# One hand-ordered queue of 513 work units, ordered anew in an attention and maxout feed-forward kernel

## The chip, the cores and the metric

The kernel runs on one core of one Trainium2 chip. The metric is device time in microseconds for one execution, the median of the runs shown. A profile is one further execution, recorded instruction by instruction.

## What is computed

Two stages in one kernel. The first is attention with batch 4, 8 heads, 768 positions and 64 channels per head. A query sees a key if the key is one of the first 8 positions ("global") or lies 0 to 95 positions behind it ("local"); a head's slope times the distance is taken off the score. The second stage multiplies each token (3072 of them, 512 channels) by three weight matrices, keeps the largest of the three products, and multiplies by a fourth matrix.

```python
scores = scale * np.matmul(q, k.transpose(0, 1, 3, 2))
keep = is_global | is_local
dist = np.where(is_global & ~is_local, float(n_local), np.abs(rel))
scores = np.where(keep, scores - slopes * dist, -1e9)
a = softmax(scores)
x = (a @ v) as [B*S, H*D]
h = np.maximum(np.maximum(x @ w1, x @ w2), x @ w3)      # 512 -> 768
out = h @ w_out                                          # 768 -> 512
```

## The kernel before

The 3072 tokens are 24 tiles of 128 (6 per batch entry). A tile's scores reach only its own keys and those of the tile before it, and the 8 global keys are copied over the first 8 columns of the earlier key tile. exp runs without a maximum; the distance and the mask are one multiplication of exp(scores) by exp(-slope x distance), from a table `wmask` built at the start (units K, one per head). V carries a column of ones, so that one matmul gives sum and denominator.

The feed-forward stage works on eight chunks: four of 2 tiles, then four of 4. For each chunk there are 18 groups F (6 blocks of 128 hidden channels times 3 matrices), each four accumulating matmuls into one PSUM buffer; ScalarE copies the first matrix's product out (j = 0), VectorE takes the maximum with the second (j = 1) and the third (j = 2). O is the second matmul of a tile, with its copy and its store.

Nothing in the kernel chooses an order at run time. A string, `SCHEDULE`, lists 513 units, and a loop issues them one after the other. An engine executes its own instructions in that order, so a unit waits for everything that stands ahead of it on its engine. A unit is a letter and numbers. The last number of many units says which engine does the copy or the multiplication: 0 ScalarE, 1 VectorE, 2 GpSimd. In `u_m` it is different, (VectorE, GpSimd) by 0 and 1:

```python
mul = (nc.vector, nc.gpsimd)[how].tensor_mul
```

The units that this text speaks of:

- `l n.s` loads a part of q or k for a group of tiles, `c n.s.e` casts it to bf16, `x n.s.e` transposes it on PE and copies it out of PSUM. Group 0 is the first four tiles in eight parts: 0 to 3 are q of head pairs 0 to 3, called q0 to q3 here, 4 to 7 are k, called k0 to k3. `L`, `C T.0`, `X` do the same for the tiles from 12 on, one tile at a time, with the transpose by DMA (last number 4) or on PE.
- `v T` loads V, `C T.1.e` casts it. `w`, `o` load weights, `W g.j.e` and `Q` cast them. All loads are issued by SP in the order of the list.
- For the first four tiles scores are made for a head pair: `s tp.jp.b` (tp 0: tiles 0 and 1; tp 1: tiles 2 and 3) is PE's scores in PSUM buffer b and ScalarE's exp, `m tp.jp.e` the mask multiplication (L344 with 768 elements per partition for tp 0, L342 with 1024 for tp 1), `g` small copies of global key columns.
- For later tiles `S T.g` and `M T.g` do the same by half of the heads (the multiplication is L360).
- `A T.b` is attention times V and the division on VectorE; with b = 2 in two halves (two PSUM buffers of the three that feed-forward groups use, two reciprocals and two divisions of half the size), else in one. `T T.e` transposes the result for the feed-forward stage, on PE with a copy by e, or by DMA (4). `G` and `V` copy global columns of K and V for a tile.
- `D b.n` issues n matmuls on zeros. `E` is the last chunk's second matmul.

The PSUM pool of the feed-forward groups (`psH`) has three buffers, which T, D and the A units with b = 2 take too, in turn; `psS` has one buffer for each of b = 0 and 1, and `psT` one.

Of the kernel before, what the change touches and what calls it, by code (L numbers as in the profile page):

```python
# [22 lines left out]


SCHEDULE = """
    K0 l0.6 K4 K2 c0.6.2 x0.6.1 K3 K5 l0.0 c0.0.2 x0.0.3 l0.4 c0.4.2 K1 x0.4.4 l0.2 c0.2.1 x0.2.3 l0.1
    g2.0.1 K7 s0.0.1 c0.1.2 s0.2.0 l0.5 c0.5.1 x0.5.4 l0.3 l0.7 c0.7.1 x0.1.3 c0.3.2 g2.2.1 K6 g1.2.2
    g1.0.2 g2.1.1 x0.3.2 x0.7.3 s0.1.1 s0.3.0 g1.1.2 s1.0.1 m0.2.0 s1.2.0 w0.0.0 g1.3.1 g2.3.1 s1.3.1 v0
    C0.1.1 m0.3.0 m0.1.0 m0.0.0 A0.2 m1.0.0 s1.1.0 v1 C1.1.2 m1.3.0 W0.0.0 A1.1 m1.1.0 m1.2.1 D5.6 T0.0
    V1.2 T1.1 v2 C2.1.2 A2.2 V2.0 F0.0.0 v3 C3.1.2 G0.0 A3.1 V3.0 w1.0.0 W2.0.2 w0.1.0 T2.0 F0.4.0  # L30
    F0.1.0 T3.0 F0.5.0 W1.0.1 W0.1.2 F0.1.1 w0.2.0 W0.2.2 l1.0 c1.0.2 G3.0 F1.0.0 F1.0.1 F1.1.0 F1.1.1
    F1.2.0 F0.1.2 F0.2.0 l1.1 c1.1.1 x1.0.2 F0.0.1 F0.0.2 x1.1.4 F1.1.2 F1.4.0 S4.0 S4.1 G4.2 F1.0.2
    F1.3.0 F1.5.0 S5.0 w1.1.0 W2.1.2 M4.0 M4.1 F0.5.1 F0.4.1 M5.0 l2.0 c2.0.0 F1.5.1 S5.1 v5 v4 C4.1.0
    W1.1.2 F0.2.1 F1.3.1 F1.4.1 M5.1 F0.3.0 x2.0.0 l2.2 c2.2.1 A4.1 w1.2.1 W1.2.0 C5.1.2 F0.3.1 x2.2.2
    F1.2.1 V4.2 A5.1 T4.1 F1.3.2 F0.2.2 S7.0 l2.3 T5.1 F1.2.2 F0.3.2 W2.2.2 F1.5.2 F2.0.0 F2.3.0 c2.3.1
    F2.1.0 x2.3.0 M7.0 F0.4.2 F2.4.0 F2.3.1 l2.1 c2.1.2 x2.1.4 F2.5.0 F2.1.1 v6 G6.0 C6.1.1 v8 C8.1.2
    S6.0 l3.0 c3.0.2 S6.1 F2.0.1 M6.0 F2.4.1 M6.1 F2.2.0 S7.1 F0.5.2 v7 C7.1.0 F1.4.2 M7.1 A6.0 F2.5.1
    x3.0.0 F2.2.1 A7.1 F2.2.2 o1 v9 T6.0 o2 Q2.2 F2.1.2 G7.0 F2.4.2 S8.1 S8.0 T7.1 F2.5.2 F2.3.2 F3.0.0
    F3.3.0 M8.0 F3.1.0 F3.4.0 F3.1.1 Q1.2 M8.1 G8.0 F3.2.0 S9.1 C9.1.1 S9.0 F3.4.1 F2.0.2 F3.1.2 V7.2
    G9.2 A8.1 l3.1 c3.1.2 v11 o0 v10 F3.5.0 x3.1.4 L12 C12.0.2 F3.0.1 L15 v15 L13 Q0.0 F3.2.1 M9.1 S10.0  # L40
    S10.1 F3.0.2 O0.1.0 L14 F3.5.1 F3.4.2 F3.2.2 M9.0 M10.0 C15.0.3 C13.0.3 V8.0 G10.0 S11.1 T8.4 S11.0
    O1.1.0 C11.1.0 X12.0 X13.4 L19 A9.1 F3.3.1 M10.1 O2.1.1 V9.2 C10.1.2 v12 C14.0.2 O0.0.0 M11.0 T9.0
    A10.1 O2.0.1 M11.1 S12.0 S12.1 G12.0 X14.4 V10.2 L16 T10.1 F3.5.2 F3.3.2 X15.4 v13 v14 L18 S13.0
    C12.1.2 S13.1 A11.2 O3.0.1 C15.1.2 M12.0 M12.1 T11.0 O3.1.1 G13.0 C19.0.1 F4.0.0 F4.0.1 F4.3.0
    F4.5.0 M13.0 A12.1 F4.5.1 S14.0 S14.1 T12.4 M14.0 M13.1 M14.1 C16.0.2 F4.4.0 F4.4.1 F4.4.2 G14.0
    S15.0 X16.4 M15.0 S15.1 F4.1.0 F4.0.2 C13.1.2 A13.0 T13.4 V13.0 M15.1 F4.2.0 F4.1.1 C14.1.2 A14.0
    V14.1 G15.2 O1.0.0 T14.4 F4.3.1 A15.1 C18.0.1 F4.2.1 V15.0 F4.2.2 F4.5.2 F4.1.2 S16.0 S16.1 G16.1
    M16.1 F4.3.2 T15.4 F5.0.0 F5.3.0 F5.3.1 F5.0.1 F5.5.0 F5.5.1 X18.4 X19.4 S19.1 S18.0 M18.0 v18 L17
    F5.2.0 F5.5.2 C17.0.1 v19 L21 M16.0 C18.1.1 F5.2.1 v16 C16.1.2 F5.2.2 F5.0.2 S18.1 M18.1 S19.0
    F5.1.0 F5.1.1 F5.1.2 X17.4 v17 M19.0 L20 L22 A16.2 S17.0 S17.1 C17.1.2 M17.1 T16.4 M19.1 G18.2  # L50
    C19.1.2 O4.0.0 A18.0 M17.0 T18.4 F5.4.0 C20.0.0 O4.3.0 X20.4 F5.4.1 C21.0.0 A19.1 T19.4 V16.2 A17.0
    T17.4 F5.3.2 F5.4.2 O4.1.1 v21 O5.3.0 O5.1.0 X21.4 G19.2 C22.0.3 X22.4 O4.2.0 L23 C23.0.2 S20.1
    S20.0 M20.0 v22 F6.0.0 M20.1 F6.0.1 F6.2.0 F6.5.0 F6.2.1 v20 C20.1.2 G20.0 S21.0 S21.1 F6.0.2 F6.1.0
    F6.1.1 G21.0 S22.0 S22.1 G22.0 X23.4 M22.0 M21.0 M21.1 O5.2.0 F6.1.2 C22.1.2 V19.0 F6.3.0 M22.1
    F6.3.1 A20.0 F6.4.0 T20.4 C21.1.2 F6.3.2 S23.0 S23.1 F6.2.2 F6.5.1 V20.2 A21.0 V21.0 v23 F6.4.1
    T21.4 F6.4.2 A22.0 T22.4 F6.5.2 O6.2.0 O6.3.0 M23.1 C23.1.2 V22.2 M23.0 A23.1 T23.4 O6.0.1 O5.0.0
    O6.1.1 F7.0.0 F7.3.0 F7.1.0 F7.2.0 F7.2.1 F7.2.2 F7.0.1 F7.4.0 F7.3.1 F7.1.1 F7.1.2 F7.0.2 F7.3.2
    F7.4.1 F7.4.2 F7.5.0 F7.5.1 F7.5.2 E
"""


# [522 lines left out]
```

## Time and profile before

| | |
|---|---|
| median of 9 runs | 184.94 us (183.8 to 186.46) |
| the profiled execution's own time | 184.69 us |
| its span, first to last instruction | 182.9 us |
| PE busy | 165.9 us, 91% |
| VectorE (DVE) busy | 125.4 us, 69% |
| ScalarE (ACT) busy | 102.8 us, 56% |
| GpSimd (POOL) busy | 43.8 us, 24% |
| mean DMA rate | 199 GB/s |
| mean granted TensorE clock | 0.978 |

Busy times are of the whole span and mix stages with different limits: the head, in which the inputs arrive and the first four tiles' attention is made, and the long part after it, in which feed-forward matmuls of early chunks lie between the attention of later tiles. A matmul's recorded duration overlaps that of the next, so a busy PE is not a PE at its peak.

### The profile page before, as it was taken

The page shows a single profiled execution, that of the slowest core. Times are in us where ns is not written, and L with a number is a line of the kernel's source. Part 1 is how long each engine was busy: PE and PEld are TensorE (multiplying, and loading weights), DVE is VectorE, ACT ScalarE, POOL GpSimd, SP SyncE. Part 2 cuts the span into 40 slices and gives each one's busy share as a digit, 9 for nine tenths or more (in the row PEclk, how much of TensorE's full clock was granted, in tenths as well). Part 3 has the DMA queues.
Part 4 walks back from the last instruction along what each step waited for, and adds up shares of the span by engine and source line. Part 5 has one row for each costly group of instructions (what it writes and reads, how often), then busy time and mean ns, then how long its engine had stood idle before and what let it go on. Part 6 is the DMA issues. An engine that isn't in the chain of part 4 may idle for free.

```text
span 182.9 us, 4085 instructions
## 1 busy us (share of the span) xinstructions
PE 165.9 (91%) x1574; PEld 102.0 (56%) x1590; DVE 125.4 (69%) x261; ACT 102.8 (56%) x174; POOL 43.8 (24%) x70
## 2 busy tenths in 40 slices
PE   0677399999999999999999999999999899999991
PEld 0356289778888866654455444554444454444451
DVE  2568956799699768787897649796066977326610
ACT  5699176895877798463752643671677342231131
POOL 6327750724250512311330000510002602000000
PEclk9996879999999999999999999999999999999998
DMA  5999999999999917999999799999898463510005
GB/s 162 306 266 266 351 295 305 291 336 244 306 264 224 218 33 185 190 312 139 235 241 164 150 233 177 218 216 169 239 228 168 115 97 107 201 61 2 0 37 192
DMA packets 85331, 36.31 MB, mean 199 GB/s; under 512 B 69440, under 2 KB 80576, under 8 KB 85312
## 3 DMA queue, kind: packets, MB, share of 16 engines
q1 hardware_dynamic: 85168, 35.99, 85.9%
q8 instruction: 12, 0.20, 0.5%
q10 hardware_dynamic: 144, 0.07, 0.1%
q14 instruction: 7, 0.06, 0.1%
HBM read 25.17 MB, written 6.29 MB: 172 GB/s over the span
## 4 chain that ended last, share of the span: by engine, by line
PE 75%; DVE 10%; ACT 6%; DMA 4%; issue 3%; SPq 0%; POOL 0%; ACTq 0%
PE h L428 45%; PE po L448 15%; PE sp L292 5%; PE op L377 3%; DVE P L360 3%; DMA rawp<-in_k_dram 3%; PE op L380 2%; ACT P L296 2%; DVE P L342 2%; PE tpp L250 2%; ACT P L332 2%; DVE xb L396 2%; PE xtp L415 1%; DMA out_dram<-ost 1%; DVE P L344 1%
## 5 line engine op out<-in xcount | busy, mean ns | idle before, releaser
L428 PE MATMUL h<-xT,w 128*128 128x256 bf16 (+1 forms) x564 | 101.9, 326 | 1.2 <-DVE h01s L439 0.2
L428 PEld LDWEIGHTS <-w 128*128 128x128 bf16 x576 | 53.9, 98 | 35.7 <-issue 1.1
L296 ACT ACTIVATE P<-sp 128x1024 bf16<-128x1024 f32 (+1 forms) x40 | 36.5, 961 | 16.3 <-PE sp L292 16.2
L448 PE MATMUL po<-wo,ht 128*128 128x512 bf16 (+2 forms) x152 | 33.0, 362 | 0.2
L360 DVE TENSOR_TENSOR P<-P,wmask 128x1024 bf16<-128x1024 bf16 x34 | 26.1, 785 | 8.9 <-ACT P L296 8.8
L437 ACT CAST h<-h 128x512 bf16<-128x512 f32 x24 | 14.1, 588 | 20.8 <-PE h L428 20.5
L439 DVE TENSOR_TENSOR h<-h,h 128x512 bf16<-128x512 bf16 x24 | 16.4, 685 | 11.6 <-PE h L428 11.5
L454 ACT COPY ost<-po 128x512 f32<-128x512 f32 (+2 forms) x18 | 9.9, 558 | 22.2 <-PE po L448 15.2
L448 PEld LDWEIGHTS <-ht 128*128 128x128 bf16 x156 | 14.2, 98 | 14.7 <-DVE ht L441 0.3
L200 POOL CAST va<-rawv 128x512 bf16<-128x512 f32 x16 | 11.6, 733 | 36.6 <-DMA rawv<-in_v_dram 34.8
L441 DVE TENSOR_TENSOR ht<-h,h 128x512 bf16<-128x512 bf16 x24 | 16.1, 684 | 3.7 <-PE h L428 2.9
L377 PEld LDWEIGHTS <-P 128*128 128x128 bf16 x192 | 13.5, 102 | 3.5 <-DVE P L344 0.7
L250 PE MATMUL tpp<-identb,qkp 128*128 128x128 bf16 x96 | 9.2, 248 | 6.0 <-POOL qkp L194 5.9
L396 DVE TENSOR_TENSOR xb<-op,rz 128x512 bf16<-128x512 f32 x20 | 13.8, 691 | 0.7
L377 PE MATMUL op<-va,P 128*128 128x65 bf16 x160 | 13.4, 200 | 0.7 <-DVE P L342 0.5
L439 DVE TENSOR_TENSOR h01s<-h01s,h 128x256 bf16<-128x256 bf16 x24 | 9.6, 415 | 5.5 <-PE h L428 2.7
L292 PE MATMUL sp<-qkT 64*128 64x128 bf16 x296 | 12.1, 218 | 0.4 <-DVE xb L396 0.3
L292 PEld LDWEIGHTS <-qkT 64*128 64x128 bf16 x296 | 8.3, 94 | 7.1 <-issue 6.2
L380 PEld LDWEIGHTS <-P 128*128 128x128 bf16 x160 | 11.4, 102 | 1.4 <-issue 0.4
L437 ACT CAST h01s<-h 128x256 bf16<-128x256 f32 x24 | 8.9, 375 | 5.9 <-PE h L428 4.5
L441 DVE TENSOR_TENSOR ht<-h01s,h 128x256 bf16<-128x256 bf16 x24 | 9.7, 418 | 2.4 <-PE h L428 2.2
L250 PEld LDWEIGHTS <-qkp 128*128 128x128 bf16 x96 | 7.0, 110 | 7.6 <-POOL qkp L194 6.4
(82 smaller groups left out, 147.5 us busy)
## 6 DMA issues: line engine op xcount, KB each, us to landing
rawv<-in_v_dram SPq DMA_DIRECT2D x24, 256.0 KB, 5.3
out_dram<-ost SPq DMA_DIRECT2D x23, 256.0 KB, 3.0
raw<-in_q_dram SPq DMA_DIRECT2D x12, 256.0 KB, 5.0
raw<-in_k_dram SPq DMA_DIRECT2D x12, 256.0 KB, 5.1
wst<-in_moe_w_dram SPq DMA_DIRECT2D x5, 512.0 KB, 7.0
wst<-in_moe_w_dram SPq DMA_DIRECT2D x2, 1024.0 KB, 8.6
rawp<-in_q_dram SPq DMA_DIRECT2D x4, 512.0 KB, 8.1
rawp<-in_k_dram SPq DMA_DIRECT2D x4, 512.0 KB, 7.2
```

The costliest lines, as they stand in the source:

```text
L250: nc.tensor.transpose(tp[:, e, j - lo], qb["p", n, s][:, e, 2 * j:2 * j + 2].rearrange("i h d -> i (h d)"), identb)
L292: nc.tensor.matmul(sp[:, hh, j2, ds], qT(T - ds, 1)[hsl, jp], qT(T, 0)[hsl, jp], start=True, stop=True, skip_group_check=True)
L296: nc.scalar.activation(P[:, :, 0:n], sp.rearrange("p a b d n -> p (a b) d n")[:, :, 0:n], AF.Exp, bias=0.0, scale=scale)
L360: nc.vector.tensor_mul(P, P, wmask[:, g, :, 1:3])
L377: nc.tensor.matmul(o, get_P(T, g, j2, hh, 0), heads(va[T])[:, h], start=True, stop=(t == 0), skip_group_check=True)
L380: nc.tensor.matmul(o, get_P(T, g, j2, hh, 1), heads(va[T - 1])[:, h], start=False, stop=True, skip_group_check=True)
L396: nc.vector.tensor_tensor(out=x4, in0=o4[:, :, :, 0:64], in1=rz[:, :, :, None].to_broadcast([128, 2, 4, D]), op=ALU.mult)
L428: nc.tensor.matmul(ps, w123[f // 2][:, dm, j, (f % 2) * 128:(f % 2) * 128 + 128], xT[B][:, dm, o], start=(dm == 0), stop=(dm == 3))
L437: nc.scalar.copy(h01, ps)
L439: nc.vector.tensor_max(h01, h01, ps)
L441: nc.vector.tensor_max(ht[B][:, f, o], h01, ps)
L448: nc.tensor.matmul(po, ht[BIG[c]][:, f, lo:lo + 128], wo[:, f, cols], start=(f == 0), stop=(f == NF - 1))
```

## The change

Only the string changes. It holds the same units, in another order, and 98 of the units get another last number (another engine, or another PSUM buffer); `D5.6` becomes `D5.3`. A short description given with it reads "All mask multiplications of the first four tiles on VectorE, none on GpSimd; whole queue ordered anew with the first parts landing later". In the strings, the mask units of the first four tiles are m0.0 to m1.3: before, `m1.2.1` alone is on GpSimd; after, `m0.0.1` and `m1.0.1` are.

The strings' beginnings, in which the first four tiles are made and the feed-forward stage begins, the lines with S6 and A6 and with T8, and the ends:

```diff
@@ -23,39 +23,39 @@
 SCHEDULE = """
-    K0 l0.6 K4 K2 c0.6.2 x0.6.1 K3 K5 l0.0 c0.0.2 x0.0.3 l0.4 c0.4.2 K1 x0.4.4 l0.2 c0.2.1 x0.2.3 l0.1
-    g2.0.1 K7 s0.0.1 c0.1.2 s0.2.0 l0.5 c0.5.1 x0.5.4 l0.3 l0.7 c0.7.1 x0.1.3 c0.3.2 g2.2.1 K6 g1.2.2
-    g1.0.2 g2.1.1 x0.3.2 x0.7.3 s0.1.1 s0.3.0 g1.1.2 s1.0.1 m0.2.0 s1.2.0 w0.0.0 g1.3.1 g2.3.1 s1.3.1 v0
-    C0.1.1 m0.3.0 m0.1.0 m0.0.0 A0.2 m1.0.0 s1.1.0 v1 C1.1.2 m1.3.0 W0.0.0 A1.1 m1.1.0 m1.2.1 D5.6 T0.0
-    V1.2 T1.1 v2 C2.1.2 A2.2 V2.0 F0.0.0 v3 C3.1.2 G0.0 A3.1 V3.0 w1.0.0 W2.0.2 w0.1.0 T2.0 F0.4.0
-    F0.1.0 T3.0 F0.5.0 W1.0.1 W0.1.2 F0.1.1 w0.2.0 W0.2.2 l1.0 c1.0.2 G3.0 F1.0.0 F1.0.1 F1.1.0 F1.1.1
-    F1.2.0 F0.1.2 F0.2.0 l1.1 c1.1.1 x1.0.2 F0.0.1 F0.0.2 x1.1.4 F1.1.2 F1.4.0 S4.0 S4.1 G4.2 F1.0.2
-    F1.3.0 F1.5.0 S5.0 w1.1.0 W2.1.2 M4.0 M4.1 F0.5.1 F0.4.1 M5.0 l2.0 c2.0.0 F1.5.1 S5.1 v5 v4 C4.1.0
-    W1.1.2 F0.2.1 F1.3.1 F1.4.1 M5.1 F0.3.0 x2.0.0 l2.2 c2.2.1 A4.1 w1.2.1 W1.2.0 C5.1.2 F0.3.1 x2.2.2
-    F1.2.1 V4.2 A5.1 T4.1 F1.3.2 F0.2.2 S7.0 l2.3 T5.1 F1.2.2 F0.3.2 W2.2.2 F1.5.2 F2.0.0 F2.3.0 c2.3.1
-    F2.1.0 x2.3.0 M7.0 F0.4.2 F2.4.0 F2.3.1 l2.1 c2.1.2 x2.1.4 F2.5.0 F2.1.1 v6 G6.0 C6.1.1 v8 C8.1.2
-    S6.0 l3.0 c3.0.2 S6.1 F2.0.1 M6.0 F2.4.1 M6.1 F2.2.0 S7.1 F0.5.2 v7 C7.1.0 F1.4.2 M7.1 A6.0 F2.5.1
...
-    S10.1 F3.0.2 O0.1.0 L14 F3.5.1 F3.4.2 F3.2.2 M9.0 M10.0 C15.0.3 C13.0.3 V8.0 G10.0 S11.1 T8.4 S11.0
...
-    O6.1.1 F7.0.0 F7.3.0 F7.1.0 F7.2.0 F7.2.1 F7.2.2 F7.0.1 F7.4.0 F7.3.1 F7.1.1 F7.1.2 F7.0.2 F7.3.2
-    F7.4.1 F7.4.2 F7.5.0 F7.5.1 F7.5.2 E
+    K0 l0.6 K6 c0.6.0 l0.0 K5 l0.4 c0.0.1 x0.0.3 c0.4.0 K2 l0.2 c0.2.1 x0.6.1 K4 K7 x0.2.2 l0.5 c0.5.1
+    x0.4.2 g2.0.1 x0.5.0 g2.2.1 s0.2.0 m0.2.0 g1.2.1 l0.3 c0.3.2 s0.0.1 g2.1.1 x0.3.2 l0.1 c0.1.2 x0.1.3
+    K3 l0.7 c0.7.2 x0.7.1 K1 s0.1.1 m0.1.0 g1.0.0 s0.3.0 s1.0.1 g2.3.1 g1.3.0 s1.2.0 m0.3.0 v0 C0.1.2
+    m0.0.1 A0.2 v1 C1.1.2 A1.2 m1.0.1 m1.2.0 g1.1.0 s1.1.0 m1.1.0 s1.3.1 w0.1.0 v2 w0.0.0 W0.0.0 v3
+    C3.1.0 w1.0.0 T0.1 m1.3.0 T1.1 D5.3 C2.1.2 V1.2 A2.2 V2.2 F0.0.0 A3.0 F0.1.0 W0.1.2 F0.0.1 W2.0.0
+    T2.1 V3.2 w0.2.0 T3.0 l1.0 F0.1.1 F0.5.0 F1.0.0 F1.1.0 W1.0.2 F0.2.0 F1.4.0 W0.2.1 F0.1.2 l1.1
+    c1.1.1 G0.2 F1.2.0 G3.2 c1.0.2 x1.0.2 F1.1.1 F0.0.2 x1.1.4 F1.1.2 S4.0 S4.1 F1.0.1 F1.0.2 M4.0
+    F0.4.0 G4.2 F1.5.0 S5.0 S5.1 M4.1 w1.1.0 W1.1.2 W2.1.1 F0.2.1 F1.2.1 M5.0 F1.3.0 v5 C5.1.2 v4 F0.5.1
+    C4.1.2 F1.4.1 F1.5.1 A4.0 l2.0 c2.0.0 F0.3.0 x2.0.0 F1.3.1 l2.2 c2.2.2 M5.1 w1.2.1 F0.4.1 W1.2.0
+    x2.2.2 l2.3 T4.1 F0.3.1 V4.2 A5.1 F1.3.2 F1.2.2 W2.2.0 S7.0 l2.1 T5.1 F0.3.2 F0.4.2 c2.3.1 M7.0
+    F2.0.0 F2.4.0 F2.3.0 F2.0.1 x2.3.0 F1.5.2 G6.0 F2.4.1 F2.4.2 c2.1.2 x2.1.4 F2.3.1 F2.0.2 S7.1 S6.0
+    F1.4.2 M6.0 F2.1.0 F2.1.1 S6.1 M6.1 F2.3.2 M7.1 l3.0 c3.0.2 v6 C6.1.0 F2.5.0 F0.5.2 A6.0 G7.0 v7
...
+    S10.0 M10.0 S10.1 G10.0 L13 T8.1 L15 L18 F3.2.0 Q0.2 O1.1.1 M10.1 F3.2.1 C12.0.0 C11.1.0 M9.1 C9.1.2
...
+    O6.3.0 O5.2.0 F7.0.0 F7.4.0 F7.2.0 F7.0.1 F7.0.2 F7.1.0 F7.5.0 F7.1.1 F7.5.1 F7.1.2 F7.3.0 F7.2.1
+    F7.4.1 F7.4.2 F7.3.1 F7.2.2 F7.3.2 F7.5.2 E
 """
```

The last number of the units changes for 11 A, 23 C, 10 G, 10 O, 2 Q, 6 T, 13 V, 5 W, 5 c, 4 g, 3 m and 6 x units. Of the transposes by DMA one goes to PE and VectorE (`T8.4` to `T8.1`). The order of the loads in SP's queue changes: of the first eight parts, the fifth to seventh (q1, k1, q3 become k1, q3, q1); then `w0.0 v0 v1 v2 v3 w1.0 w0.1 w0.2` becomes `v0 v1 w0.1 v2 w0.0 v3 w1.0 w0.2`; and later V and tile loads trade places.

More of the change, by code (lines that the diff above doesn't have):

```diff
@@ L36 @@
-    F2.1.0 x2.3.0 M7.0 F0.4.2 F2.4.0 F2.3.1 l2.1 c2.1.2 x2.1.4 F2.5.0 F2.1.1 v6 G6.0 C6.1.1 v8 C8.1.2
-    S6.0 l3.0 c3.0.2 S6.1 F2.0.1 M6.0 F2.4.1 M6.1 F2.2.0 S7.1 F0.5.2 v7 C7.1.0 F1.4.2 M7.1 A6.0 F2.5.1
-    x3.0.0 F2.2.1 A7.1 F2.2.2 o1 v9 T6.0 o2 Q2.2 F2.1.2 G7.0 F2.4.2 S8.1 S8.0 T7.1 F2.5.2 F2.3.2 F3.0.0
-    F3.3.0 M8.0 F3.1.0 F3.4.0 F3.1.1 Q1.2 M8.1 G8.0 F3.2.0 S9.1 C9.1.1 S9.0 F3.4.1 F2.0.2 F3.1.2 V7.2
-    G9.2 A8.1 l3.1 c3.1.2 v11 o0 v10 F3.5.0 x3.1.4 L12 C12.0.2 F3.0.1 L15 v15 L13 Q0.0 F3.2.1 M9.1 S10.0
@@ L41 @@
-    S10.1 F3.0.2 O0.1.0 L14 F3.5.1 F3.4.2 F3.2.2 M9.0 M10.0 C15.0.3 C13.0.3 V8.0 G10.0 S11.1 T8.4 S11.0
[L42 to L55, printed above, removed]
@@ L56 @@
-    T21.4 F6.4.2 A22.0 T22.4 F6.5.2 O6.2.0 O6.3.0 M23.1 C23.1.2 V22.2 M23.0 A23.1 T23.4 O6.0.1 O5.0.0
-    O6.1.1 F7.0.0 F7.3.0 F7.1.0 F7.2.0 F7.2.1 F7.2.2 F7.0.1 F7.4.0 F7.3.1 F7.1.1 F7.1.2 F7.0.2 F7.3.2
-    F7.4.1 F7.4.2 F7.5.0 F7.5.1 F7.5.2 E
+    K0 l0.6 K6 c0.6.0 l0.0 K5 l0.4 c0.0.1 x0.0.3 c0.4.0 K2 l0.2 c0.2.1 x0.6.1 K4 K7 x0.2.2 l0.5 c0.5.1
+    x0.4.2 g2.0.1 x0.5.0 g2.2.1 s0.2.0 m0.2.0 g1.2.1 l0.3 c0.3.2 s0.0.1 g2.1.1 x0.3.2 l0.1 c0.1.2 x0.1.3
+    K3 l0.7 c0.7.2 x0.7.1 K1 s0.1.1 m0.1.0 g1.0.0 s0.3.0 s1.0.1 g2.3.1 g1.3.0 s1.2.0 m0.3.0 v0 C0.1.2
@@ new lines @@
+    C4.1.2 F1.4.1 F1.5.1 A4.0 l2.0 c2.0.0 F0.3.0 x2.0.0 F1.3.1 l2.2 c2.2.2 M5.1 w1.2.1 F0.4.1 W1.2.0
+    x2.2.2 l2.3 T4.1 F0.3.1 V4.2 A5.1 F1.3.2 F1.2.2 W2.2.0 S7.0 l2.1 T5.1 F0.3.2 F0.4.2 c2.3.1 M7.0
+    F2.0.0 F2.4.0 F2.3.0 F2.0.1 x2.3.0 F1.5.2 G6.0 F2.4.1 F2.4.2 c2.1.2 x2.1.4 F2.3.1 F2.0.2 S7.1 S6.0
+    F1.4.2 M6.0 F2.1.0 F2.1.1 S6.1 M6.1 F2.3.2 M7.1 l3.0 c3.0.2 v6 C6.1.0 F2.5.0 F0.5.2 A6.0 G7.0 v7
+    F2.2.0 C7.1.2 x3.0.2 A7.1 F2.2.1 F2.2.2 o2 T6.0 S8.0 S8.1 F0.2.2 V7.0 T7.1 F2.5.1 F2.5.2 M8.0 v12
@@ new lines @@
+    C12.1.1 F3.0.0 F3.4.0 v8 C8.1.1 F3.5.0 G8.2 S9.0 S9.1 G9.2 l3.1 c3.1.2 o1 Q2.0 Q1.2 F3.4.1 F3.0.1
+    F3.4.2 M8.1 F3.5.1 v10 C10.1.1 o0 F2.1.2 F3.1.0 x3.1.0 A8.0 L12 v11 v9 L14 F3.5.2 F3.3.0 F3.3.1 M9.0
+    S10.0 M10.0 S10.1 G10.0 L13 T8.1 L15 L18 F3.2.0 Q0.2 O1.1.1 M10.1 F3.2.1 C12.0.0 C11.1.0 M9.1 C9.1.2
+    S11.0 S11.1 V8.2 M11.0 C14.0.0 C13.0.2 X13.4 F3.2.2 O2.1.0 X14.4 O0.1.0 A9.0 C15.0.2 v13 X15.4 V9.1
+    X12.0 G12.2 F3.3.2 F3.0.2 O0.0.1 A10.1 V10.0 L16 M11.1 F3.1.1 F3.1.2 O2.0.1 T10.0 S12.1 S12.0 A11.2
@@ new lines @@
+    v15 T9.1 M12.1 M12.0 v14 O3.0.0 L19 S13.0 S13.1 G13.0 T11.1 O1.0.1 F4.0.0 F4.5.0 A12.1 F4.0.1
+    C13.1.2 F4.5.1 S14.1 C18.0.1 S14.0 G14.1 M13.0 F4.5.2 O3.1.0 M14.1 M13.1 S15.1 S15.0 F4.4.0 C16.0.2
+    F4.4.1 M14.0 F4.3.0 A13.0 V13.2 T12.4 T13.4 F4.0.2 F4.4.2 C14.1.0 M15.0 A14.1 V14.2 M15.1 X16.4
+    T14.4 C15.1.0 F4.3.1 F4.1.0 F4.1.1 A15.0 V15.2 G15.1 F4.1.2 C19.0.0 T15.4 F4.2.0 F4.2.1 F4.2.2
+    F4.3.2 S16.1 M16.1 X19.4 S16.0 M16.0 X18.4 F5.0.0 F5.5.0 F5.5.1 F5.3.0 F5.5.2 S18.0 S19.1 M19.1 L17
@@ new lines @@
+    C17.0.2 M18.0 v16 C16.1.2 F5.2.0 F5.0.1 F5.2.1 L20 C20.0.3 S18.1 S19.0 X17.4 F5.2.2 F5.3.1 M19.0
+    G16.0 F5.1.0 F5.0.2 M18.1 F5.3.2 F5.1.1 A16.2 S17.0 M17.0 v18 C18.1.0 v19 S17.1 X20.4 M17.1 v17 L21
+    F5.4.0 C19.1.2 T16.4 L22 O4.0.0 F5.4.1 A19.0 C17.1.0 F5.1.2 V16.0 F5.4.2 A17.1 T19.4 A18.0 G18.0
+    T18.4 T17.4 O5.3.0 V19.1 v20 G19.1 C20.1.2 C21.0.1 O4.2.1 X21.4 L23 S20.1 C23.0.2 C22.0.0 X22.4
+    S20.0 M20.0 v21 X23.4 O4.1.0 G20.0 v23 O4.3.1 v22 O5.1.0 M20.1 F6.0.0 F6.3.0 F6.3.1 A20.0 V20.2
@@ L59 @@
+    F6.3.2 T20.4 F6.2.0 S21.1 S21.0 F6.1.0 F6.0.1 F6.2.1 G21.2 S22.0 M21.1 M22.0 S22.1 F6.0.2 F6.1.1
+    C21.1.0 F6.1.2 M22.1 M21.0 G22.0 F6.4.0 S23.0 S23.1 F6.4.1 C22.1.2 F6.5.0 F6.5.1 A21.1 T21.4 F6.5.2
+    F6.2.2 V21.2 F6.4.2 A22.1 V22.1 M23.0 T22.4 M23.1 O6.0.0 O6.2.0 C23.1.2 A23.1 T23.4 O5.0.0 O6.1.1
+    O6.3.0 O5.2.0 F7.0.0 F7.4.0 F7.2.0 F7.0.1 F7.0.2 F7.1.0 F7.5.0 F7.1.1 F7.5.1 F7.1.2 F7.3.0 F7.2.1
+    F7.4.1 F7.4.2 F7.3.1 F7.2.2 F7.3.2 F7.5.2 E
 """
```

## Prediction

> **What bounds the kernel now.** I read the page first, its slices by engine and granted clock, then the busy time by stage.
>
> ```profile
> PE   0677399999999999999999999999999899999991
> PEclk9996879999999999999999999999999999999998
> ...
> PE 75%; DVE 10%; ACT 6%; DMA 4%; issue 3%; SPq 0%; POOL 0%; ACTq 0%
> ```
> ```profile
> 15.00:20.00 5.00, 2.99 (x44) 2.46 (x42) 4.44 (x8) 3.71 (x5) 3.92 (x5) 0.70 1.01 318
> 20.00:25.00 5.00, 3.52 (x46) 3.15 (x47) 3.71 (x11) 1.29 (x5) 3.02 (x3) 0.66 1.18 309
> 25.00:30.00 5.00, 5.00 (x51) 4.47 (x50) 2.80 (x7) 3.23 (x10) 1.31 (x2) 1.00 1.03 338
> ...
> 140.00:160.00 20.00, 19.31 (x157) 9.82 (x158) 14.22 (x24) 7.15 (x13) 4.44 (x7) 1.00 0.51 124
> ```
> The columns of a stage are its length, then the busy time of PE, PE's weight load, DVE, ACT and POOL, the granted clock, DMA share and GB/s. From 25 us on TensorE is the bound. From 30 to 160 us the stages add up to 128.1 us of PE in 130, so all waits of the dense part cost 1.9 us, 0.69 of them after 140. What an order can still win is mostly the head, up to 25 us, where PE is busy half the time and its clock falls to 0.66. Next the chain of waits in the head:
>
> ```profile
> 13.55 1.92 DVE P L344 x3
> 15.47 0.05 issue
> 15.52 0.41 PE op L377 x4
> ...
> 17.14 2.88 DVE P L342 x2
> 20.03 0.13 DVE rz L395
> 20.16 0.02 issue
> 20.18 0.69 DVE xb L396
> 20.87 1.08 DVE P L342
> 21.95 0.05 issue
> 22.00 0.24 PE op L377
> ```
> From 13.55 to 21.95 VectorE is the path: masks of tiles 0 and 1 (L344), attention 0 (A0, 15.52), two masks of tiles 2 and 3 (L342), the rest of attention 1, the last mask; then A2, and the first feed-forward group at 22.65. The rows of the two mask lines, as min/median/max ns:
>
> ```profile
> L344 DVE TENSOR_TENSOR P<-P,wmask x4: 548/554/964, 12.0 to 14.5; 128x768 bf16<-128x768 bf16 x4
> ```
> ```profile
> L342 DVE TENSOR_TENSOR P<-P,wmask x3: 1044/1150/1993, 17.1 to 20.8; 128x1024 bf16<-128x1024 bf16 x3
> L342 POOL TENSOR_TENSOR P<-P,wmask x1: 2122/2122/2122, 15.4 to 15.4; 128x1024 bf16<-128x1024 bf16 x1
> ```
> The timelines show why one instruction varies so much. The 0.96 us one starts at 14.50, during a GpSimd cast from 14.29 to 15.06; the 1.99 us one runs from 18.03, during GpSimd's copy and casts from 17.74 to 19.48. The like multiplication of later tiles (L360) takes 0.68 us where GpSimd rests.
>
> **What the Trainium skill says.** GPSIMD Engine Reference, section "8. Key points", says that GpSimd shares its SBUF interfaces with VectorE and contends with VectorE instructions that have two SBUF inputs. The trace agrees: 0.55 alone, 0.96 beside a cast. The same page, "4.1 Engine selection", puts a two-input operation on GpSimd at about twice VectorE's time; here 2.12 us against 0.68 clean and 1.04 to 1.99 contended. TensorE: Matmul & The Clock Gate, "What's actually happening", says that the clock is set by PE's activity in free-running windows of about 3.4 us. The trace agrees: half clock from about 14.6 to 18.0 and 21.4 to 24.8 us, each after a thin stretch.
>
> **What the change does, read from the diff.** Its short description says that GpSimd gets no mask multiplication. The diff says otherwise: the last number of a unit m is the engine (0 VectorE, 1 GpSimd). Before, GpSimd has m1.2; after, it has m0.0 and m1.0. I follow the diff. All else is order and engines: the same 513 units, 3 dummy matmuls fewer (D5, x6 at a pitch of about 0.1 us: 0.3 us in PE's idle time, worth nothing unless the clock needed them).
>
> **Loads.** All in SP's queue. The first four parts keep their places (one q part, q2, stays fourth), so k2, q0, k0, q2 land as now, at 3.5, 4.3, 6.4 and 7.2 us. Then k1, q3, q1, k3 follow, 7.9 to 10.3. w0.0 (512 KB, some 1.55 us at 330 GB/s) no longer stands ahead of v0 and v1: v0 13.04 to 11.5, v1 14.2 to 12.7. w0.1 moves between v1 and v2; v3 slips from 16.4 to about 17.9 and w0.0 to 16.8. The set up to the first 1 MB weight is the same, so that one still lands near 21.8, the next near 24.
>
> **ScalarE, walked.** Pitches from the rows: wmask 0.41, exp of 384 0.37, exp of 1024 0.91, copies from PSUM 0.48. It gains two casts (not shown at this size on ScalarE; the 512-element V cast takes 0.64, the copy pitch is 0.48; I take 0.5), one more PSUM copy and three tiny copies (0.15). K0, K6, cast k2, K5: 3.77 to 5.55. Cast k0 waits for 6.41, done 7.0. K2, K4, K7 to 8.2; copies q2, k0, k1 to 9.8; four exps to 11.3; copy q3, K3, K1 to 12.6; s0.1 exps 13.35; tiny copy; s0.3 exps 14.25; s1.0 to 15.2; s1.2 15.35 to 16.3. Now: s0.3 ends at 13.5 and the third exp of 1024 at 16.2, so the pieces for A0 come later and those for tiles 2 and 3 about as now.
>
> **Masks.** m0.2 on VectorE at 10.7 and m0.1 at 13.5, m0.3 behind it at 14.65. m0.0 on GpSimd: 2.12 x 768/1024 = 1.6 us, bounded by 0.55 and 2.12; it waits for K1, so 12.75 to 14.35, beside m0.1, which I stretch to 0.95. The v1 cast then lies beside m0.3, stretched to 0.9: A0 at 15.6, against 15.52. **Nothing gained yet.**
>
> Then VectorE: A0 to 17.2 (two halves, 0.18 + 0.42 each, as now). A1, now also in halves, follows at once and is done at 18.35, not behind two masks at 20.87. m1.0 runs on GpSimd, 15.4 to 17.5, beside A0 and A1 and not beside VectorE masks. Behind A0 and A1 in PE's queue stand s1.1 and s1.3: exps 17.8 to 19.7, against 17.74 now. VectorE: m1.2 1.0 us (C2 and V1 on GpSimd beside it) to 19.35; m1.1 0.68 to 20.0; T0's copy to 20.4; m1.3 0.68 to 21.0; T1's copy 21.3. A2's second half needs the PSUM buffer that T1's copy frees, so A2 ends at 21.7 and F0.0.0 starts then, not at 22.65. V2 (on GpSimd, 0.6, now 0.41 on ScalarE) is ready at 22.3, under F0.0.0's 0.85 us at half clock. Then A3 to 23.45, F0.1.0 and F0.0.1, still cold, to 24.9, T2, T3, F0.1.1, F0.5.0; W2.0 on ScalarE (24.7 to 25.7) and T3's copy (26.2) just precede their users. F1.0.0 at about 26.35, with 5 groups done. Now 3 are done at 26.06; two more (0.44 each) make 26.93. **Head: 0.6 us gained.**
>
> **Dense part.** PE's work is the same but for T8 (four transposes, +0.22 us, a DMA transpose less). I counted VectorE's work per 10 us of PE work with the pitches of the rows: today three crowded stretches (10.0, 9.4 and 10.0), one of them around 138 to 146 us, where the chain runs over VectorE; after, one of 10.2, the rest at most 8.6. GpSimd loses some 4 us of casts, ScalarE takes 5. I give 0.5 of the 0.69 us back, an estimate, bounds -1.2 and +2.5. The moved M, C, X, O, L units issue the same DMAs otherwise; DMA transposes get 4 us of PE work or more ahead of their scores. The tail (E, 5.4 us after the last matmul) stays.
>
> **Sum.** 184.69 (the profiled execution: span 182.9 and 1.8 around it) - 0.6 - 0.5 = 183.6. Its median is 0.25 higher (184.94): **183.8 us**.
>
> **Rivals.**
> 1. *GpSimd's mask becomes the bound of A0.* If m0.0 takes 2.12 us or K1 comes late, A0 starts at 16.6; A1, s1.1, s1.3, their exps and two masks stand behind it, since the new order puts both attentions ahead of these scores. It decides when A0 starts after 16.2; with A1 and the scores at half clock (+0.5) the head loses 0.4 to 1.0. With no dense gain: 185.8. For it: two-input work on both engines was stretched up to 3 times. Against: m0.0 has 2 us before its user.
> 2. *Given back to the loads.* l1.1 lands at 27.5 either way, ScalarE and VectorE are full from 33 to 38 us, and the gain turns into waiting before S4: 184.9.
> 3. *A dense stall.* S6.1 to A6 has 1.3 us of PE work between (2.5 now) for an exp (0.59), a mask (0.49) and their queues: up to 1.5 us: 185.8.
> 4. *Both go well*: clean masks, dense waits down by 1.2: 182.7.
> 5. *The description holds, not the diff*: m0.0 and m1.0 on VectorE add 1.2 to 1.7: 185.7.
>
> **Chances.** Likeliest 0.35, case 4 0.12: faster 0.47. Case 2 0.20: same. Case 1 0.20, case 3 0.11, case 5 0.02: slower 0.33. A measurement can tell about 0.5% (0.9 us), which bounds "same". The likeliest case's own range is 182.6 to 185; with the bounds of the unknown costs 182.3 to 187.0.
>
> **What would show it.** Right: A0 near 15.6, m1.1 and m1.3 on VectorE below 0.8 us, F0.0.0 near 21.7, PE over 19.5 of 20 us in 140 to 160. Wrong: A0 after 16.2, VectorE masks over 1 us behind A1, PE below 19.3 in any 20 us after 40.

## The result, and the profile after

| | before | after |
|---|---|---|
| median | 185.16 us (52 runs, 183.16 to 188.96) | 183.55 us (17 runs, 181.77 to 186.86) |
| the profiled execution | 184.69 us, span 182.9 | 183.05 us, span 181.3 |

The ratio is 0.9907, 95% interval [0.9877, 0.9936]: faster by some 0.9%. Ratios here leave disturbed executions out and medians do not, so the two need not agree to the last tenth. The short description's clause on the masks is not what was run: after, as the diff has it, GpSimd does two mask multiplications.

The page of after, the lines of PE and its clock and the chain by engine; then its busy time by stage:

```profile
PE   0487899899999999999999999999899999999991
...
PEclk9999999999999999999999999999999999999999
...
PE 78%; ACT 7%; DVE 6%; DMA 5%; issue 2%; SPq 1%; ACTq 0%; DVEq 0%
```
```profile
15.00:20.00 5.00, 4.33 (x60) 3.47 (x55) 4.86 (x15) 3.63 (x7) 4.45 (x4) 1.00 1.09 332
20.00:25.00 5.00, 4.51 (x60) 3.64 (x58) 4.22 (x13) 3.51 (x6) 3.08 (x6) 1.00 1.19 308
25.00:30.00 5.00, 4.66 (x51) 4.17 (x50) 2.55 (x7) 3.83 (x8) 1.19 (x1) 1.00 1.13 312
...
120.00:140.00 20.00, 19.31 (x161) 9.56 (x162) 11.64 (x23) 10.58 (x16) 2.15 (x4) 1.00 0.92 179
140.00:160.00 20.00, 19.84 (x146) 9.93 (x147) 10.82 (x20) 8.20 (x14) 1.51 (x3) 1.00 0.64 165
```
VectorE's share of the chain falls from 10 to 6%. PE no longer stands idle from 18.4 to 20.9 us, and 140 to 160 us lost 0.16 us where it lost 0.69. The clock column shows no dip, but it tells nothing of the time before 20.45 us (see the last section). But 120 to 140 us now lose 0.69, and 25 to 30 us 0.34 where they lost nothing.

Now the chain of waits in the new head, and the rows of the mask lines (min/median/max ns):

```profile
13.75 1.33 DVE P L344
15.08 0.52 DVE k2x L305
15.60 0.07 DVE k2x L306
15.67 0.47 DVE P L344
16.14 0.05 issue
16.19 0.35 PE op L377 x3
...
17.95 1.94 ACT P L332 x2
19.89 0.93 ACT w L503
20.82 0.53 ACT va L200
21.35 0.58 PE h L428 x4
```
```profile
L344 DVE TENSOR_TENSOR P<-P,wmask x3: 545/641/1333, 10.9 to 15.6; 128x768 bf16<-128x768 bf16 x3
L344 POOL TENSOR_TENSOR P<-P,wmask x1: 1635/1635/1635, 13.0 to 13.0; 128x768 bf16<-128x768 bf16 x1
```
```profile
L342 DVE TENSOR_TENSOR P<-P,wmask x3: 673/879/966, 18.2 to 20.3; 128x1024 bf16<-128x1024 bf16 x3
L342 POOL TENSOR_TENSOR P<-P,wmask x1: 2545/2545/2545, 15.6 to 15.6; 128x1024 bf16<-128x1024 bf16 x1
```
A0 is not earlier: its last operand comes at 16.14, where it came by 15.5. Its path now runs through one mask of 1.33 us, beside GpSimd's mask (13.03 to 14.67 us), and a small copy of 0.60, beside the cast of a part of V that follows on GpSimd (14.61 to 15.55). From there on the order is better. The masks of tiles 2 and 3 on VectorE take 0.67 to 0.97 us (they took 1.04 to 1.99), and the first feed-forward group starts at 21.33 us, not 22.65.

The two lines that the chain puts ahead of PE's group are ScalarE's cast of W0.0 and its cast of a part of V. The second isn't what the group waits for: it is an operand of A3, not of this group, and ends only as the group starts. The group does need T1's copy, on VectorE, which ends at 21.28 us:

```profile
20.87 0.41 DVE L416 COPY xT<-xtp 128x512 bf16<-128x512 bf16 x1
```
Five feed-forward groups of the first chunks are done at 24.92 us (24.04, where the block of 32 matmuls starts, and two groups of 0.44), against 26.93 before: 2.0 us. The profiled executions differ by 1.64. So the head gained 2.0 and the rest gave 0.4 back.

### The profile page after: what moved, and what is told of

Its sections match the earlier page's. It is cut to its first block, busy times and chain, and to the rows that moved or that the text cites. A ratio compares the mean times of both kernels' runs of the same rounds, so it can differ in the third digit from the quotient of the medians.

```text
span 181.3 us, 4087 instructions
## 1 busy us (share of the span) xinstructions
PE 165.9 (92%) x1575; PEld 102.8 (57%) x1591; DVE 122.1 (67%) x264; ACT 107.0 (59%) x178; POOL 39.8 (22%) x63
## 4 chain that ended last, share of the span: by engine, by line
PE 78%; ACT 7%; DVE 6%; DMA 5%; issue 2%; SPq 1%; ACTq 0%; DVEq 0%
PE h L428 49%; PE po L448 14%; PE sp L292 6%; PE op L377 3%; DMA rawp<-in_k_dram 3%; DMA out_dram<-ost 3%; PE op L380 2%; ACT P L332 2%; PE tpp L250 2%; DVE h01s L439 2%; PE xtp L415 1%; ACT wmask L355 1%; DVE ht L441 1%; DVE P L360 1%; DVE P L344 1%
## 5 line engine op out<-in xcount | busy, mean ns | idle before, releaser
L439 DVE TENSOR_TENSOR h<-h,h 128x512 bf16<-128x512 bf16 x24 | 16.3, 685 | 19.3 <-PE h L428 16.4
L360 DVE TENSOR_TENSOR P<-P,wmask 128x1024 bf16<-128x1024 bf16 x34 | 24.4, 729 | 5.9 <-ACT P L296 5.9
L437 ACT CAST h<-h 128x512 bf16<-128x512 f32 x24 | 14.0, 589 | 17.9 <-PE h L428 15.4
L200 POOL CAST va<-rawv 128x512 bf16<-128x512 f32 x12 | 8.2, 690 | 35.8 <-DMA rawv<-in_v_dram 30.9
L377 PEld LDWEIGHTS <-P 128*128 128x128 bf16 x192 | 13.1, 100 | 3.6 <-DVE P L344 0.7
L396 DVE TENSOR_TENSOR xb<-op,rz 128x512 bf16<-128x512 f32 x19 | 13.1, 691 | 0.7
L380 PEld LDWEIGHTS <-P 128*128 128x128 bf16 x160 | 11.1, 100 | 1.5
```

What stands on the lines that cost most here:

```text
L360: nc.vector.tensor_mul(P, P, wmask[:, g, :, 1:3])
L377: nc.tensor.matmul(o, get_P(T, g, j2, hh, 0), heads(va[T])[:, h], start=True, stop=(t == 0), skip_group_check=True)
L380: nc.tensor.matmul(o, get_P(T, g, j2, hh, 1), heads(va[T - 1])[:, h], start=False, stop=True, skip_group_check=True)
L396: nc.vector.tensor_tensor(out=x4, in0=o4[:, :, :, 0:64], in1=rz[:, :, :, None].to_broadcast([128, 2, 4, D]), op=ALU.mult)
L437: nc.scalar.copy(h01, ps)
L439: nc.vector.tensor_max(h01, h01, ps)
```

## The experiments

All ratios are to the kernel before on the same chip. In e1 to e4 line numbers are one below those of the other kernels.

**e1 and e2: head and rest apart.** Both cut behind T3. What is left of the queue follows in the other kernel's order.

```diff
# e1_head_new, behind T3.0 of the changed kernel
-l1.0 F0.1.1 F0.5.0 F1.0.0 F1.1.0 W1.0.2 F0.2.0 F1.4.0
...
+G0.0 F0.4.0 F0.5.0 W1.0.1 F0.1.1 W0.2.2 l1.0 c1.0.2
...
# e2_rest_new, behind T3.0 of the kernel before
-F0.5.0 W1.0.1 W0.1.2 F0.1.1 w0.2.0 W0.2.2 l1.0 c1.0.2
...
+W0.1.2 F0.0.1 w0.2.0 l1.0 F0.1.1 F0.5.0 F1.0.0 F1.1.0
...
```


> The new order up to T3 (both attention pairs of the first four tiles transposed), then the old order for all units that are left. Theory A (the change wins in the head alone, 2.0 us at the first feed-forward groups, and gives 0.4 back later): 2.0 us below the kernel before, ratio near 0.989. Rival B (head 0.6, dense part 0.5 or more, as the prediction had it): 0.6 us below, ratio near 0.997. In the profile A wants T3 on PE by 23.7 us and full clock from 21 us on.

> The old order up to T3, then the new order for all units that are left. Theory A: 0.4 us above the kernel before, ratio near 1.002. Rival B: 0.5 to 1.0 us below it, ratio near 0.996. In the profile A wants the first feed-forward group near 22.6 us, as before.

e1 measured 0.9883 [0.983, 0.9936] (median 182.84 us), e2 1.011 [1.0065, 1.0155] (187.01). The gain is the head's alone, as theory A had it, and Rival B, the prediction's own split, falls. But the new rest behind the old head costs 2.0 us, not 0.4. The timelines of e2 (VectorE, GpSimd, PE) and then of after (VectorE, GpSimd) show the spot:

```profile
36.46 1.52 DVE L502 CAST w<-wst 128x1024 bf16<-128x1024 f32 x1
```
```profile
35.94 1.49 POOL L193 CAST qkp<-rawp 128x1024 bf16<-128x1024 f32 x1
```
```profile
38.36 1.47 PE L427 MATMUL h<-xT,w 128*128 128x256 bf16 x12 [1.72 <-DVE h01s L438]
```
```profile
34.38 0.68 DVE L503 CAST w<-wst 128x1024 bf16<-128x1024 f32 x1
```
```profile
35.94 1.29 POOL L194 CAST qkp<-rawp 128x1024 bf16<-128x1024 f32 x1 [2.01 <-DMA rawp<-in_k_dram]
```
Behind the new head the weight cast W2.1 on VectorE is over before GpSimd gets its part of k, which lands when it lands. Behind the old head it comes 2.1 us later and meets that cast; both stretch, and PE waits 1.72 us for the maximum queued behind it.

**e8: that one cast back on GpSimd.**

```diff
# against e2_rest_new
-W2.1.1
+W2.1.2
```


> The kernel of e2_rest_new with one weight cast (W2.1) on GpSimd, as in the kernel before, and not on VectorE. In e2 it took 1.52 us on VectorE from 36.46 us, beside a cast of the next k part on GpSimd, and PE stood 1.72 us behind it. Theory E (this meeting of two casts is most of what the new rest costs behind the old head): the wait goes down to 0.5 us or less, 1.2 us or more below e2, ratio to before near 1.004. Rival (the wait is VectorE's load as a whole, or moves to the next cast on GpSimd): time within 0.5 us of e2, ratio 1.008 to 1.012.

1.0046 [1.0023, 1.0069], median 185.80: 1.2 us below e2, as theory E said. The wait on PE's timeline is 0.71 us, not the 0.5 or less that was expected:

```profile
38.36 1.47 PE L428 MATMUL h<-xT,w 128*128 128x256 bf16 x12 [0.71 <-DVE h01s L439]
```
So one cast, late by 2 us, made by the medians some 1.2 of the 2.0 us that the new rest cost. The evidence is not the strongest: the two intervals, from different chips, just touch, and the two profiled executions took the same 186.61 us, since e8's reached this stretch 1.0 us later, with full clock at 26.27 us and not 24.17. The new rest suits the new head better than the old one.

**e3 and e4: the masks.**

```diff
# e3_masks_vector
-m0.0.1
+m0.0.0
-m1.0.1
+m1.0.0
# e4_m00_first: m0.0 moved ahead of s0.1
-K1 s0.1.1 m0.1.0
+K1 m0.0.0 s0.1.1 m0.1.0
...
-m0.0.1 A0.2 v1
+A0.2 v1
```


> The changed kernel with m0.0 and m1.0 on VectorE in their places, as the short description has it. Rival 5's price in the prediction: 1.2 to 1.7 us above the changed kernel (ratio to before near 0.998). Theory C (a multiplication on GpSimd costs VectorE about as much as it takes off it: m0.1 took 1.33 us beside m0.0 and 0.55 alone, small copies 0.6 for 0.2): A2's last mask ends near 20.8 us instead of 20.94, time within 0.5 us of the changed kernel, ratio to before 0.988 to 0.992.

> The changed kernel with m0.0 on VectorE and moved ahead of s0.1, where VectorE waits a microsecond for the next exp. Theory C: m0.1 falls from 1.33 to 0.55 us, A0 starts near 15.2 us instead of 16.2, and all that stands behind it comes up to 0.8 us earlier: ratio to before near 0.986. Rival D (ScalarE's exps, which end at 19.8 us, and not A0 set the head's end): A0 earlier, first feed-forward group unchanged near 21.3, time as the changed kernel, 0.991.

e3: 0.9884 [0.9844, 0.9923], median 182.78. With every mask on VectorE the kernel is no slower than the changed one. A0 starts at 15.25 us, 0.9 us earlier than in the changed kernel although VectorE has one mask more ahead of it, and the first group at 21.10. The lines of A0 and of the masks of tiles 2 and 3:

```profile
15.25 0.62 PE L376 MATMUL op<-vaf,P 128*128 128x65 bf16 x8 [0.67 <-DVE P L343]
```
```profile
L341 DVE TENSOR_TENSOR P<-P,wmask x4: 683/684/687, 17.9 to 20.0; 128x1024 bf16<-128x1024 bf16 x4
```
Four clean masks take 2.74 us on VectorE. In the changed kernel three take 2.52, and GpSimd works 2.55 us besides. Theory C holds: GpSimd's help takes nothing off the path here.

e4: 0.9875 [0.9835, 0.9915], median 183.24. A0 now runs from 15.06 to 15.4 us and the first group starts at 20.80, half a microsecond earlier, so Rival D falls on the head. The time hardly moved, though. The records of the granted clock name a reason: full clock at 24.32 us, against 20.45 in the profile of after. In e4 the next two groups took 1.7 us from 22.51 to 24.2; after's took about 1.0. The lines of e4, then of after (a recorded duration reaches into the next matmul):

```profile
20.80 1.01 PE L427 MATMUL h<-xT,w 128*128 128x256 bf16 x4
22.51 1.89 PE L427 MATMUL h<-xT,w 128*128 128x256 bf16 x8
```
```profile
21.33 0.60 PE L428 MATMUL h<-xT,w 128*128 128x256 bf16 x4
22.30 1.15 PE L428 MATMUL h<-xT,w 128*128 128x256 bf16 x8
```

**e5: dummies to keep PE busy.**

```diff
# against e4_m00_first
+D6.4 behind each of s0.1.1, s0.3.0, s1.0.1, s1.2.0
-D5.3
+D5.10
```


> The kernel of e4_m00_first with four matmuls on zeros behind each of s0.1, s0.3, s1.0 and s1.2, where PE waits for ScalarE, and ten in place of three behind T1. Theory F (how early the clock is released is a good part of what the head still costs: full clock came at 20.45 us in the profile of the changed kernel, only at 24.32 in that of e4, where the 13th feed-forward matmul started at 24.99 against 24.04 although the first was 0.5 us earlier): full clock before 20 us, 1.0 us or more below e4, ratio to before near 0.981. Rival G (the dummies stand in the way of scores, or the window's phase decides alone): time of e4 or up to 0.5 us above, 0.988 to 0.991.

0.9814 [0.9774, 0.9853], median 181.46: below both kernels, and 1.8 us below e4 by the medians, though these two intervals overlap a little. Full clock came at 16.20 us. The dummies did stand in the way a little: A0 starts at 15.93, and the first group at 21.19, later than e4's. All the same two groups and both transposes behind A3 are through by 23.89 (e4: 24.99), and the six runs lie between 180.65 and 182.25, where the changed kernel's 17 spread from 181.77 to 186.86. Against the profile of after, in which full clock came early too, the same point is only 0.15 us earlier (23.89 and 24.04), so the profiles do not show what brings e5's median 2.1 us below after's; that full clock comes late in many executions of after would fit its spread, but only one of them was recorded. The masks are clean too, though in part by their later place:

```profile
L342 DVE TENSOR_TENSOR P<-P,wmask x3: 681/684/686, 18.6 to 20.1; 128x1024 bf16<-128x1024 bf16 x3
```

**e10: the same dummies in the kernel before.**

```diff
# against before
+D6.4 behind each of s0.1.1, s0.3.0, s1.0.1, s1.2.0
+D6.20 between T0.0 and T1.1
```


> The kernel before with the same dummies: four matmuls on zeros behind each of s0.1, s0.3, s1.0, s1.2, and twenty between T0 and T1, where PE waited 2.5 us. Theory F (the clock is a part of its own, and a thin stretch of PE in the old order took it away): full clock from about 18 us on, no half clock at 21.4 to 24.8, where the first group and A3 cost 0.9 us more than at full clock; 0.6 to 1.0 us below before, ratio near 0.996. Rival: the old order's PE work there waits for VectorE anyway, clock or not: within 0.3 us of before, ratio 0.998 to 1.002.

0.9959 [0.9928, 0.999]; the median of all 22 runs, 185.26, is not below before's. The ratio is the expected one, but the profile does not show the mechanism: full clock stood until 20.92, and then came half clock to 24.33 all the same.

```profile
17.50:20.90 3.40, 1.13 (x21) 0.96 (x19) 3.37 (x5) 1.21 (x2) 2.66 (x5) 1.00 1.09 363
20.90:24.30 3.40, 3.28 (x42) 2.87 (x43) 2.31 (x6) 0.90 (x3) 2.39 (x3) 0.50 1.20 300
```
PE was busy 1.13 of 3.4 us in the stretch ahead of it, dummies and all: twenty at full clock are over too soon for a wait of this length. So whether the old order could keep its clock is not settled.

**e7 and e12: attention 1 early, and two casts off GpSimd.**

```diff
# e7_a1_early, against before
-A0.2 m1.0.0 s1.1.0 v1 C1.1.2 m1.3.0 W0.0.0 A1.1 m1.1.0
+A0.2 v1 C1.1.2 A1.2 m1.0.0 s1.1.0 m1.3.0 W0.0.0 m1.1.0
# e12_a1_casts, against e7
-C3.1.2
+C3.1.0
-W2.0.2
+W2.0.0
```


> The kernel before with one move: v1, C1.1 and A1 directly behind A0, A1 in two halves as in the changed kernel; mask engines, loads and the rest as before. Theory A2 (the gain of the head comes from attention 1 no longer standing behind two masks of tiles 2 and 3 on VectorE): its division ends near 18.3 us instead of 20.87, the first feed-forward group starts near 21.4 us instead of 22.65, 1.0 to 1.3 us below before: ratio near 0.994. Rival H (s1.1, now behind A1 on PE, and the last exp become the bound): its exp ends near 19 us instead of 17.74, the group starts at 22.3 us or later, ratio 0.998 or above.

> The kernel of e7_a1_early with two casts (C3.1 and W2.0) on ScalarE, as in the changed kernel, and not on GpSimd. In e7 the three masks on VectorE behind attention 1 took 1.39, 0.68 and 1.53 us, the long ones beside casts on GpSimd. Theory C: the last falls to about 0.7 us, the first group starts near 21.3 us instead of 22.08, 0.7 us below e7, ratio near 0.993. Rival (ScalarE's queue holds up the group instead): no change, 0.997.

e7: 0.997 [0.9945, 0.9995]. Attention 1's division ends at 18.29 us, as theory A2 said. But the first group starts at 22.08, not 21.4: about half of what the changed kernel wins there. The rows of e7 and then e12 show what is missing:

```profile
L342 DVE TENSOR_TENSOR P<-P,wmask x3: 677/1393/1526, 18.2 to 20.1; 128x1024 bf16<-128x1024 bf16 x3
```
```profile
L342 DVE TENSOR_TENSOR P<-P,wmask x3: 679/680/833, 18.4 to 19.7; 128x1024 bf16<-128x1024 bf16 x3
```
With the casts on ScalarE the three masks take 2.2 us, not 3.6, and the first group starts at 21.13. For the start of the group that is theory C, and with A1 it makes up the whole move from 22.65 to 21.3. The time did not follow: 1.000 [0.9964, 1.0036], median 187.12. C3.1 stood behind the first group's copy on ScalarE and was done at 23.1 us, A3 waited 1.0 us for it, and W2.0 then held up the next group by 1.0 us. The clock added to it: it came full at 31.10 us in this profile, and nine feed-forward groups in a row took 5.74 us from 27.74, where the same nine took 4.09 us in the kernel before (from 25.91). The times run from 184.17 to 188.74; the profile is of an execution of 187.3 us, and the ratio rests on those of at most 186.49, for which no profile shows when full clock came. The expectation of 0.993 missed, at least in part by where I put the casts in ScalarE's queue, which the changed kernel does not share.

**e11: the loads alone.**

```diff
# against before
-w0.0 v0 v1 v2 v3 w1.0 w0.1 w0.2
+v0 v1 w0.1 v2 w0.0 v3 w1.0 w0.2
```


> The kernel before with the new order of the loads between v0 and w0.2 alone (v0 v1 w0.1 v2 w0.0 v3 w1.0 w0.2). VectorE's cast of v0 waited 0.26 us for its data and A0 for a mask held up behind that cast: A0 up to 0.3 us earlier, ratio 0.998 to 1.000. Rival (v3 and w0.0 land 1.5 and 5 us later and hold up A3 or the first group): ratio above 1.002.

1.0008 [0.9983, 1.0032]. No effect that can be measured, either way.

**e6 and e9: the better head with the old rest.**

```diff
# e6_mixed: e4 up to T3, e9_best: e5 up to T3, then
-l1.0 F0.1.1 F0.5.0 F1.0.0 F1.1.0 W1.0.2 F0.2.0 F1.4.0
...
+G0.0 F0.4.0 F0.5.0 W1.0.1 F0.1.1 W0.2.2 l1.0 c1.0.2
...
```


> The order of e4_m00_first up to T3, then the old order for the rest: the better head with the better rest. If the two add up: 0.4 us below e4, as the head of e1 was 0.4 us below the changed kernel: ratio near 0.984. If the rest eats what the head brings (loads that land at 27.2 us either way): ratio as e1, 0.988.

> The head of e5_warm (m0.0 early on VectorE, dummies behind the scores) up to T3, then the old order for the rest. The measured steps, added up: e5 stands at 0.981, the old rest behind the new head was 0.4 us better than the new one (e1 against the changed kernel), 0.0 to 0.4 behind e4's (e6): ratio 0.979 to 0.981. If loads set the pace by now (l1.1 lands near 27.2 us, x1.1 needs it): no gain over e5, 0.981 to 0.983.

e6: 0.9872 [0.9827, 0.9918], inside e4's interval; nothing added up that can be told. e9: 0.9932 [0.9906, 0.9958], a clear miss, 2.6 us above e5 by the medians. Its head is as good as e5's (third group on PE at 22.3 us against 22.7), so the loss is later. From 120 to 160 us PE stands idle for 1.85 us in e9's profile and 0.32 in e5's, and e9 has PE waiting for DMA transposes there, which do not hold up PE's matmuls in e5:

```profile
PEld L292 <- DMA qkT<-qkb: 1.9, 2, 1.2
PEld L428 <- DMA xT<-xb: 1.4, 1, 1.4
PE sp L292 <- DMA qkT<-qkb: 1.0, 2, 0.7
PE h L428 <- DMA xT<-xb: 0.9, 1, 0.9
```
The scores that wait are those of tile 21 (0.70 us, at 134.05) and of tile 23 (0.26, at 144.55); the transposes in that stretch landed 4.0 to 4.8 us after their issue, and 3.1 to 4.5 in e6, which has the same rest and one such wait of 0.35 us. Why the two differ is open, and so is what makes up the rest of the 2.6 us: it is one profile.

## Why the prediction was right, and where not

Time, side and range held: 183.8 us forecast, 183.55 measured. The working behind it held in part.

- **ScalarE and the loads**: the walk was good to about 0.3 us (s0.1's exps at 12.78, predicted 12.6; s1.2 starting at 15.42, predicted 15.35), with every part of q and k landing 0.2 us later than in the profile of before.
- **A0 at 15.6** failed: 16.2. The terms are m0.1 beside m0.0, sized 0.95 us and measured 1.33, and the small copies behind it, 0.59 us where the walk left 0.2; m0.1 also began 0.25 us later, and m0.3, sized 0.9, took only 0.55. GpSimd's own price was right (1.6, measured 1.635); what it takes from VectorE was too small. A0 came just at rival 1's threshold of 16.2, but by another way: GpSimd's mask itself was done at 14.67. It did not decide, since A1 and the masks behind it were as good as predicted.
- **Behind A0**: A1 done at 18.3 (predicted 18.35), m1.1 0.88 (0.68, beside a copy on GpSimd), m1.3 0.67, T1's copy done at 21.3 (21.3). The first group at 21.33 beats the 21.7, because A2's second half was not as late: it began at 20.40, behind T0's copy (to 20.35), and did not wait for T1's, as the walk had it. e7 and e12 split the move of the group's start: A1 ahead of the masks gave 0.57 us, the casts off GpSimd another 0.95, together a little more than the changed kernel's 1.32.
- **Clock**: the step that failed most. I kept half clock from 21.4 to 24.8, as before. In the profile of after full clock stands from 20.45. From the start of the first group to the end of the third the walk has 3.2 us; it took 2.1. That is 1.1 of the 1.4 us by which five groups were done earlier than the walk had it (24.92, not 26.35), and the main reason why 0.6 was too little. Against the kernel before, the first group and A3 took 0.58 and 0.53 us by the chain, where they took 0.85 and 0.88: 0.6 of the head's 2.0 us. The prediction had no reason for keeping the half clock but that it had been so before.
- **Dense part**: wrong in sign, as far as can be told. I gave it -0.5; it costs 0.4 behind the new head (the profiles, and e1 against after, two intervals that overlap) and 2.0 behind the old one. My count of VectorE work per 10 us saw one crowd less, and 140 to 160 us did win 0.5; but 120 to 140 us, at 19.31 us of PE, came down to the sign of being wrong (19.3), and the count could not see that W2.1 moved to VectorE in the fullest stretch, nor what it meets there behind the old head (e2, e8).
- **Rival 5** named a price, 1.2 to 1.7 us for masks on VectorE. e3 shows none: I had counted the added VectorE time and not the contention that goes with it.
- **Rivals 2, 3 and 4**: A6 is not among the longer waits, and the gain was not lost to l1.1, which landed at 27.2 us. Rival 4 wanted fewer waits in the dense part, and there were more; its 182.7 is 0.85 us off.

Two mis-sized terms of opposite sign cancelled in large part: the head won 1.4 us more than forecast, the rest lost 0.9 more. That the forecast came within 0.3 us is luck; the number was better than its working.

## What to carry to other kernels

Before giving GpSimd a share of elementwise work, add what it takes from VectorE: here a 1.6 us mask saved VectorE 0.55 us and cost it more (against e3, the other mask took 1.33 us and not 0.56, and a copy 0.60 and not 0.19, beside a cast that the mask had pushed back), so VectorE alone was no slower. Put instructions with two inputs in SBUF (not PSUM) on VectorE where GpSimd rests, and GpSimd's work beside VectorE's work on PSUM: A0's and A1's divisions took 0.42 us beside GpSimd's mask (after) and without it (e3). In a head in which PE waits for others, matmuls on zeros in its waiting time can be worth a try (e5 lies 1.8 us below e4 by the medians; e10 shows that it is no certain gain). And an order that was tuned whole is better moved whole: here its second half fitted the timing of its first.

## What the runs showed that was not expected

- The clock's column on the page is 1.00 ahead of the first record of a change, and this need not be so. In after it shows 1.00 from 16 to 17 us, and the chain of waits has A1's matmuls 0.05 us apart, then A3's 0.03:

```profile
16.81 0.05 PE op L377
16.86 0.06 PE op L380
...
22.13 0.03 PE op L380
22.16 0.03 PE op L377
```
- Full clock for good came at 24.79 us (before), 20.45 (after), 19.72 (e1), 24.17 (e2), 24.73 (e3), 24.32 (e4), 16.20 and 16.11 (e5 and e9, with dummies), 17.74 (e6) and 31.10 (e12), and in the others between 24.3 and 26.3. Periods of half clock last 3.41 us or a multiple. One period more costs up to half of that, an estimated 1.7 us, where PE has work throughout: as much as the whole change. Each of these times is from one execution of a kernel.
- Contention is not only for instructions with two inputs. Two small VectorE copies of after (0.16 and 0.18 us in the kernel before), and the GpSimd cast beside the second of them:

```profile
9.76 0.59 DVE L306 COPY k2x<-qkT 128x8 bf16<-128x8 bf16 x1
15.00 0.60 DVE L305 COPY k2x<-qkT 128x120 bf16<-128x120 bf16 x1
14.61 0.94 POOL L200 CAST va<-rawv 128x512 bf16<-128x512 f32 x1
```
The stretch is a wait for the other's end. The second copy ends at 15.60 us, the cast at 15.55; the first at 10.35, and the cast that it began beside (from 9.71) at 10.33. A copy that began ahead of that cast, at 9.65, took 0.19. The weight cast of e2 ends at 37.98, 0.55 us behind the k cast on GpSimd (37.43). It looks as if the two engines take turns by whole instructions, the first to begin going first; this is read from a few places in the traces, and no run was made to test it.
